# An adaLN, multi-query attention and GELU MLP block: first rows of maxima by TensorE transposes, a lead of 16 maxima in place of 24, and half of two query groups moved into the loop

## The chip, the cores and the metric

The kernel runs on one core of one Trainium2 chip, in one launch. The metric is the device time of that launch in microseconds; 1562.04 us is the median of the runs before the change.

## What is computed

The input x is 2048 rows of 512 numbers. Six modulation vectors come from `silu(c) @ w_mod`. Two sublayers follow, each on a layer norm of x with a modulation:

```python
h = layernorm(x) * (1 + ca) + sa
q = (h @ wq) in 32 heads of 16;  k = h @ wk;  v = h @ wv      # one key and one value head for all
x = x + ga * (softmax(q k^T / 4) v, heads side by side) @ wo
h = layernorm(x) * (1 + cb) + sb
x = x + gb * (gelu(h @ w1 + b1) @ w2 + b2)                     # w1: 512 x 1376
```

All is float32 outside. Inside, most factors are split into two parts of a shorter format (names ending in H and L), and a product is three matmuls: H·H, L·H, H·L.

## The kernel before

**Units.** The rows are cut into 8 blocks of 256, and the 32 heads into 8 groups of 4. A unit is one group of heads in one block: 64 units, numbered `u`, eight units to a block. For each unit the kernel needs the maximum over the keys of each score row, then the exponentials of the scores less that maximum, then their product with the values.

**Maxima.** A step of the maxima (`Max.step`) is one score product `m` on one half of the array (64 rows), and a `tensor_reduce` on VectorE that reads the 512 scores from PSUM (lines L507 and L512). A unit has 32 steps; `m` has three PSUM banks. The steps run ahead of the exponentials by a lead: `LEAD = 6` means 24 steps. `FIRST_MAX` is the order of the first 64 steps, those of units 0 and 1 (kc is the quarter of the keys). When a unit's last step is reduced, `put_max` closes the unit: VectorE reduces over the four quarters (`mm`, L560) and transposes (`turned`, L561), GpSimd gathers (`mt`, L555) and splits (`mh`, `ml`), and four small DMAs (L550) write the result into rows 48, 49, 112 and 113 of the unit's query tile `qst`. Those rows meet rows of -1 in `ks`, so that the next score product `e` (L612) has the maximum taken off, and ScalarE's exponential (L616, `p`) needs no bias. For unit 0 two of the four DMAs go through ScalarE's queue. The first `e` of a unit cannot start before these DMAs have landed.

**The loop.** After a prologue (layer norm, keys, values, the first two of sixteen query groups, `SLOTS` giving its order by hand) comes a loop of 256 iterations, four to a unit. An iteration has two half cycles; in each, TensorE issues four `e`, four `m` and, where there is one, one half of a batch of other products, and then 16 products of the exponentials with the values (`acc`, L633). Python's `clock` counts 4 to an iteration. `later(n, fn)` issues `fn` n clocks on. Every engine runs its own queue in the order in which the Python code issues, and SyncE's queue (SP) issues nearly all DMAs, in order, each waiting where it must.

**Batches.** Jobs in a queue (`put_off`) give one batch to an iteration: first the remaining query groups (`qproj_late`), then each block's output projection and MLP (`rest`, products `wops`, `tp`, `w1ps`, `w2ps`). An iteration that gets no batch is plain. The last iterations, without maxima, are called bare in the code. `rest` of block 0 can start when unit 7 is finished, its sums are fetched back and normalized; that is tied to clock 129 and what follows from it.

**Preparation of w2.** Beside this, the weights are prepared piece by piece: w1, then wo, then w2 (`prep_w2`, 11 pieces). The code for w2 starts when every query group is sent (`state["q"] == 0`), one step at the end of an iteration; while block 0's layer norm and modulation run, `busy` holds it back, and afterwards it takes two steps at a time (`turns`):

```python
if state["mods"] and state["q"] == 0 and w2H is None: ... preps["w2"] = prep_w2()
if clock[0] >= prepared[0] + PREP and weights and weights[0] in preps and not state["busy"]:
    prepared[0] = clock[0]
    for _ in range(state["turns"]):
        ... next(preps[weights[0]], 0)
```

Step i splits piece i-1 on GpSimd (L1137 and the two lines of `split`) and loads piece i+1 through SP (L1134). The last piece, number 10, is smaller than its tile, so GpSimd clears the tile first (`memset`, L1133) and its DMA waits for that.

Of the kernel before, what the change touches and what calls it, by code (L numbers as in the profile page):

```python
# [8 lines left out]
F32 = mybir.dt.float32  # L9
F32R = mybir.dt.float32r  # L10
AF = mybir.ActivationFunctionType
ALU = mybir.AluOpType
# [12 lines left out]
SLOTS = ((2, "keys 1", "keys 1"), (2, "keys 1", "keys 1"), (2, "low 1", "heads 2"), (2, "heads 2", "k 1"), (1, "warm"), (1, "heads 2"), (2, "heads 2", "v 0"),  # L25
# [4 lines left out]
MAX_WAIT = (1, 4)  # L30
QBUFS = 4
PREP = 4
BUSY = 5
# [12 lines left out]
def raw(ap):  # L46
    return ap.bitcast(F32)
# [3 lines left out]
def adaln_mqa_mlp(  # L51
# [105 lines left out]
    def mm3(ps, pairs, every=0, cost=0, begin=True, end=True):  # L157

        n, last = 0, 3 * len(pairs) - 1
        for wh, wl, xh, xl in pairs:  # L160
            for a, b_ in ((wh, xh), (wl, xh), (wh, xl)):
                nc.tensor.matmul(ps, a, b_, start=begin and n == 0, stop=end and n == last)  # L162
                n += 1
                if every and n % every == 0:
                    yield cost
# [248 lines left out]
            nc.tensor.transpose(pv_[:, t, :], vt[32:64, t * P:(t + 1) * P], ident[32:64, 32:64])  # L414
        nc.scalar.copy(va[:, b * QT:(b + 1) * QT, 0:Dh], pv_[:, :, 16:32])

    def send_q(b, g, qH, qL):
        for t, src in enumerate((qH, qL)):
            nc.sync.dma_start(out=dq[b][g][t].rearrange("a r j n -> (a r j) n"), in_=raw(src))
        state["q"] -= 1  # L420
        sent.add((b, g))

    sent = set()

    def qpairs(b, g):
        hH, hL = hts[b]
        gs = slice(g * P, (g + 1) * P)
        return [(wqH[:, k, gs], wqL[:, k, gs], hH[:, k, :], hL[:, k, :]) for k in range(KD)]

    def qtiles(b, g):  # L430
        qH = att.tile([P, BQ], F32R, name=f"qH{b}_{g}", tag="xH", bufs=2)
        qL = att.tile([P, BQ], F32R, name=f"qL{b}_{g}", tag="xL", bufs=2)
        return qH, qL

    def qproj(b, g):

        ps = psum.tile([P, BQ], F32, name=f"qps{b}_{g}", tag="v" if g else "x")
        yield from mm3(ps, qpairs(b, g), 3, 1)
        qH, qL = qtiles(b, g)
        if g == 0:  # L440
            nc.scalar.copy(qH, ps)
            nc.vector.tensor_tensor(out=qL, in0=ps, in1=raw(qH), op=ALU.subtract)
        else:
            q32 = pro.tile([P, BQ], F32, name=f"q32_{b}_{g}", tag="h32", bufs=4)
            nc.scalar.copy(q32, ps)
            split(qH, qL, q32, act, pool)
        send_q(b, g, qH, qL)
        yield -2

    def qproj_late(b, g):  # L450
        ps = psum.tile([P, BQ], F32, name=f"qps{b}_{g}", tag="x")
        size_ = BATCH if (b, g) < LONG else SHORT
        yield from batches(ps, qpairs(b, g), size_)
        q32 = wts_pool["rest"].tile([P, BQ], F32, name=f"q32_{b}_{g}", tag="ot", bufs=2)
# [4 lines left out]
        qH, qL = qtiles(b, g)  # L459
        split(qH, qL, q32, nc.gpsimd, nc.gpsimd)  # L460
        later(4, lambda: send_q(b, g, qH, qL))


    units = [(b, Q) for b in range(len(blocks)) for Q in range(NQ)]
# [3 lines left out]
    def load_q(u):  # L468

        b, Q = units[u]  # L470
        r0, w = blocks[b]
        qst = qsts[u] = qbufs[u % QBUFS]
        h, g, a0 = r0 // BQ, Q // 2, (Q % 2) * 2
        cols = slice(r0 % BQ, r0 % BQ + w)
        assert (h, g) in sent
        for s in range(2):
            for r, part in ((0, 0), (16, 1), (32, 0)):
                nc.sync.dma_start(out=raw(qst[64 * s + r:64 * s + r + 16]), in_=dq[h][g][part, a0 + s][:, :, cols])
            if u >= QBUFS:
                nc.sync.dma_start(out=raw(qst[64 * s + 48:64 * s + 50]), in_=dz)  # L480

    class Max:


        def __init__(self):
            def products(u, kcs):
                return [(u, j, t, kc) for kc in kcs for j in range(2) for t in range(blocks[units[u][0]][1] // P)]
# [5 lines left out]
            begin = [o for u, kc in FIRST_MAX for o in products(u, [kc])]  # L493
# [37 lines left out]
    def put_max(u, mx):  # L531

        T = blocks[units[u][0]][1] // P
        qst = qsts[u]
        mm = mms[u % 2]
        turned = att.tile([P, 32], F32, name=f"turned{u}", tag="turned", bufs=2)
        if u == 0:
            pad(att, 256, "pad7")  # L540
        mt = att.tile([4 * T, P], F32, name=f"mt{u}", tag="mt", bufs=2)
        mh = att.tile([4 * T, P], F32R, name=f"mh{u}", tag="mh", bufs=2)
        ml = att.tile([4 * T, P], F32R, name=f"ml{u}", tag="ml", bufs=2)

        def send():
            for s in range(2):
                for r, src in ((48, mh), (49, ml)):
                    dst = qst[64 * s + r:64 * s + r + 1].rearrange("p j (t n) -> p (j t) n", n=P)
                    ring = nc.scalar if u == 0 and s else nc.sync
                    ring.dma_start(out=raw(dst), in_=raw(src[2 * T * s:2 * T * (s + 1), :].unsqueeze(1)))  # L550
            placed.add(u)

        def gather():
            for g in range(0, P, 32):
                nc.gpsimd.tensor_scalar(out=mt[:, g:g + 32], in0=turned[g:g + 4 * T, :], scalar1=1.0, scalar2=0.0,  # L555
                                        op0=ALU.mult, op1=ALU.add)
            split(mh, ml, mt, nc.gpsimd, nc.gpsimd)

        def reduce():
            nc.vector.tensor_reduce(out=mm[:, :4 * T], in_=mx, axis=AX.X, op=ALU.max)  # L560
# [670 lines left out]
    def q_group():  # L1231
        for i in range(KD):
            next(projections[0])
            if i == KD - 1:
                next(projections.pop(0))
            yield

    def warm():
        keep_warm(WARM[2], tag="x")
        yield  # L1240

    def one(fn, *args):
        fn(*args)
        yield
# [37 lines left out]
    def last_h(t):  # L1282
        if t == QT - 1:
# [7 lines left out]
    keep_warm(WARM[1])  # L1291
    work = {"keys 1": keys(1), "heads 2": heads(2), "heads 3": heads(3), "q 1": q_group(), "keys 2": keys(2), "keys 3": keys(3),
            "v 0": one(v_out, 0), "v 1": one(v_out, 1), "v 2": one(v_out, 2), "v 3": one(v_out, 3), "rows": late_rows(),
            "low 1": one(low_k, 1), "low 2": one(low_k, 2), "low 3": one(low_k, 3), "k 1": one(repeat_k, 1), "k 2": one(repeat_k, 2), "k 3": one(repeat_k, 3), "load": one(load_q, 2), "warm": warm(),
            "wq 1": one(prep_wq, 1), "wq 2": one(prep_wq, 2), "wq 3": one(prep_wq, 3)}
    for n, *names in SLOTS:
        chunk(n)
# [9 lines left out]
    nc.scalar.copy(mod_state["rows"], mod_state["ps"])  # L1307
    put_off(*late, late_mods(), *[qproj_late(b, g) for b in range(2, NB) for g in range(KD)])
# [212 lines left out]
```

## Time and profile before

| | us |
|---|---|
| median of 3 runs | 1562.04 (1561.88 to 1562.45) |
| the profiled execution | 1561.89 |
| its span | 1560.1 |
| TensorE busy | 1543.2 (99%) |
| VectorE busy | 1400.8 (90%) |
| ScalarE busy | 1227.4 (79%) |
| GpSimd busy | 681.5 (44%) |

The profiled execution's time is 1.8 us more than its span. Lines are those of the kernel file, engines are named PE (TensorE), PEld (its weight loads), DVE (VectorE), ACT (ScalarE), POOL (GpSimd) and SP (SyncE); SPq and ACTq rows are DMA issues. A row of the timeline has a start, a duration, the engine, the line, the operation with output and input tiles, a count where several in a row are merged, and in brackets the idle time before it and what ended it.

### The profile page before, as it was taken

The numbers are of one execution on the slowest core, as the hardware profiler recorded it, in microseconds if no ns is written. First come the engines' busy times: TensorE is split into PE (matmuls) and PEld (weight loads), VectorE is DVE, ScalarE is ACT, GpSimd is POOL, SyncE is SP. The second block draws the span as 40 slices with busy tenths as digits, with TensorE's granted clock in tenths as the row PEclk, the third lists the DMA queues.
The fourth block names the chain that finished last, engine by engine and source line by source line (L and its number), as shares of the span: only waits on it lengthen the run. The fifth ranks groups of instructions, "written<-read, shape, count | busy, mean of one in ns | idle before, by whom it ended". The sixth has DMA issues, their size and how long they took to land.

```text
span 1560.1 us, 41350 instructions
## 1 busy us (share of the span) xinstructions
PE 1543.2 (99%) x16347; PEld 955.2 (61%) x16347; DVE 1400.8 (90%) x2479; ACT 1227.4 (79%) x2392; POOL 681.5 (44%) x1194
## 2 busy tenths in 40 slices
PE   7999999999999999999999999999999999999999
PEld 4456555567655665557655675556655676556657
DVE  7999999999999999999999999999999999999725
ACT  5577778788878887788877887788877888778953
POOL 5545433867322570246522562245611474225721
PEclk9999999999999999999999999999999999999999
DMA  7225412312030211202012120302112120211241
GB/s 250 92 93 197 148 56 85 124 52 97 19 109 19 83 59 36 94 28 99 30 54 76 55 86 23 109 14 100 44 49 80 46 97 17 84 55 63 84 159 52
DMA packets 83125, 121.61 MB, mean 78 GB/s; under 512 B 19614, under 2 KB 56222, under 8 KB 82676
## 3 DMA queue, kind: packets, MB, share of 16 engines
q1 hardware_dynamic: 82916, 118.97, 22.9%
q8 instruction: 129, 2.11, 0.6%
q14 instruction: 64, 0.52, 0.1%
q10 hardware_dynamic: 16, 0.00, 0.0%
HBM read 91.13 MB, written 27.27 MB: 76 GB/s over the span
## 4 chain that ended last, share of the span: by engine, by line
PE 84%; DVE 10%; issue 3%; POOL 2%; DMA 1%; ACT 1%; SPq 0%; POOLq 0%; DVEq 0%
PE acc L633 28%; PE m L507 24%; PE e L612 15%; DVE mx L512 8%; PE w1ps L193 8%; PE w2ps L183 2%; PE w1ps L183 1%; DMA xt<-in_A_x_dram 1%; PE w2ps L193 1%; PE qps L193 1%; PE tp L193 1%; PE wops L193 1%; PE kps L162 1%; DVE st L840 1%; DVE x L833 1%
## 5 line engine op out<-in xcount | busy, mean ns | idle before, releaser
L512 DVE TENSOR_REDUCE mx<-m 128x1 f32<-128x512 f32 x2048 | 1269.3, 681 | 87.7 <-PE m L507 64.7
L616 ACT ACTIVATE p<-e 128x512 f32<-128x512 f32 x2048 | 1098.0, 598 | 254.8 <-PE e L612 106.4
L507 PE MATMUL m<-ks,qst 64*128 64x512 f32 x2048 | 832.9, 429 | 2.0 <-DVE mx L512 0.6
L612 PE MATMUL e<-qst,ks 64*128 64x512 f32 x2048 | 739.9, 413 | 0.0
L633 PE MATMUL acc<-p,va 128*32 128x256 f32 x8192 | 548.0, 385 | 0.0
L507 PEld LDWEIGHTS m<-ks,qst 64*128 64x128 f32 x2048 | 367.1, 184 | 211.6 <-DVE mx L512 174.0
L612 PEld LDWEIGHTS e<-qst,ks 64*128 64x128 f32 x2048 | 358.7, 185 | 92.3 <-ACT p L616 64.0
L633 PEld LDWEIGHTS acc<-p,va 128*32 128x32 f32 x8192 | 214.5, 109 | 213.7 <-issue 110.7
L555 POOL TENSOR_SCALAR mt<-turned 8x32 f32<-8x32 f32 x256 | 53.1, 208 | 419.5 <-DVE turned L561 407.4
L193 PE MATMUL w1ps<-h2H,w1t 64*128 64x256 f32 x1216 | 232.7, 287 | 0.0
L193 PEld LDWEIGHTS w1ps<-h2H,w1t 64*128 64x128 f32 x1216 | 183.6, 185 | 28.4 <-issue 14.4
L193 PE MATMUL w1ps<-h2L,w1t 64*128 64x256 f32 x608 | 167.0, 275 | 0.0
L193 PE MATMUL w2ps<-w2H,gH 64*128 64x512 f32 x264 | 115.9, 439 | 0.0
L193 PEld LDWEIGHTS w1ps<-h2L,w1t 64*128 64x128 f32 x608 | 112.8, 185 | 0.0
L193 PE MATMUL w2ps<-w2L,gH 64*128 64x512 f32 x264 | 103.4, 392 | 0.0
L193 PE MATMUL w2ps<-w2H,gL 64*128 64x512 f32 x264 | 103.0, 390 | 0.0
L959 POOL TENSOR_SCALAR tt<-tt 128x256 f32<-128x256 f32 x77 | 31.0, 403 | 143.1 <-ACT tt L958 109.8
L137 POOL TENSOR_TENSOR gL<-z,gH 128x256 fp32r<-128x256 f32 x77 | 56.9, 739 | 6.4
L960 POOL TENSOR_TENSOR tt<-tt,z 128x256 f32<-128x256 f32 x77 | 56.8, 738 | 6.4
L970 POOL TENSOR_TENSOR z<-tt,z 128x256 f32<-128x256 f32 x77 | 56.4, 733 | 6.0
L969 POOL TENSOR_TENSOR tt<-tt,z 128x256 f32<-128x256 f32 x77 | 56.5, 734 | 0.0
L193 PE MATMUL wops<-woH,onH 64*128 64x512 f32 x112 | 49.8, 444 | 0.0
(190 smaller groups left out, 1495.3 us busy)
## 6 DMA issues: line engine op xcount, KB each, us to landing
w1t<-dw SPq DMA_DIRECT2D x82, 512.0 KB
qst<-dq SPq DMA_DIRECT2D x384, 32.0 KB
do<-oc SPq DMA_DIRECT2D x64, 128.0 KB
dw<-w1s SPq DMA_DIRECT2D x11, 512.0 KB
xt<-in_A_x_dram SPq DMA_DIRECT2D x4, 1024.0 KB
dq<-qH SPq DMA_DIRECT2D x16, 256.0 KB
dq<-qL SPq DMA_DIRECT2D x16, 256.0 KB
x<-in_A_x_dram SPq DMA_DIRECT2D x8, 512.0 KB
```

Of the source, the lines that this page charges most:

```text
L137: eng_l.tensor_tensor(out=dst_l, in0=src, in1=raw(dst_h), op=ALU.subtract)
L183: nc.tensor.matmul(ps, a, b_, start=first_, stop=last_)
L193: ins = nc.tensor.matmul(ps, a[rows], b_[rows], start=first_ and s == 0, stop=last_ and s == 1)
L507: nc.tensor.matmul(m, qsts[u][rows, j, t * P:(t + 1) * P], ks[rows, kc * 512:(kc + 1) * 512], start=True, stop=True)
L512: nc.vector.tensor_reduce(out=self.mx[u][:, i, kc:kc + 1], in_=m, axis=AX.X, op=ALU.max)
L555: nc.gpsimd.tensor_scalar(out=mt[:, g:g + 32], in0=turned[g:g + 4 * T, :], scalar1=1.0, scalar2=0.0, op0=ALU.mult, op1=ALU.add)
L612: nc.tensor.matmul(e, ks[rows, kt * P:(kt + 1) * P], rhs, start=True, stop=True)
L616: ins = nc.scalar.activation(dst, e, AF.Exp, scale=0.25)
L633: ins = nc.tensor.matmul(accs[u][32 * cidx:32 * cidx + 32, :], va[:, kt, :], rhs, start=kt == 0, stop=kt == NKT - 1)
L960: nc.gpsimd.tensor_tensor(out=tt, in0=tt, in1=z, op=ALU.mult)
L969: nc.gpsimd.tensor_tensor(out=tt, in0=tt, in1=z, op=ALU.mult)
L970: nc.gpsimd.tensor_tensor(out=z, in0=tt, in1=z, op=ALU.add)
```

## The change

- The lead is 16 steps (`LEAD = LEAD_0 = 4`), and `FIRST_MAX` puts two of unit 1's steps behind unit 0's last, which is now step 46 and not 48. Before the loop 48 steps are issued and not 56, and five idle matmuls before the loop (`WARM[3]`) are gone.
- Unit 0 is closed without GpSimd and DMAs: VectorE writes its maxima, split in two, into columns of a cleared tile `spots`, four TensorE transposes turn that into a PSUM bank, and VectorE adds the bank to `qst`.
- The other units are closed at the next half cycle: the reduction is issued 1 clock after the last step (3 before), the gather with it (1 clock later before), the DMAs 2 clocks after that (4 before). With the shorter lead the DMAs are issued at the same clock before the unit's first `e` as before.
- The first two query groups are computed in the prologue for 256 of their 512 rows only. The other halves become two more jobs of one batch each, third and fourth in the loop's queue.

```diff
-LEAD = 6
-LEAD_0 = 6
-FIRST_MAX = ((0, 0), (1, 0), (0, 1), (1, 1), (0, 2), (0, 3), (1, 2), (1, 3))
+LEAD = 4
+LEAD_0 = 4
+FIRST_MAX = ((0, 0, 4), (1, 0, 4), (0, 1, 4), (1, 1, 3), (0, 2, 4), (0, 3, 4), (1, 1, 1), (1, 2, 4), (1, 3, 4))
...
-         (0, "v 2"), (2, "q 1"), (2, "q 1"), (2, "q 1"),
-         (2, "q 1", "rows"), (2, "v 3", "wq 2"), (2, "rows"), (2, "rows"), (2, "rows", "wq 3", "load"))
-MAX_WAIT = (1, 4)
+         (0, "v 2", "q 1", "q 1", "spots"), (2, "q 1", "q 1"), (2, "q 1"), (2, "rows", "wq 2"), (2, "wq 3"),
+         (2, "rows", "load"), (2, "v 3", "rows", "first", "rows"))
+MAX_WAIT = 2
-WARM = (4, 16, 2, 5)
+WARM = (4, 16, 2, 0)
-    state = {"mods": False, "q": NB * KD, "busy": False, "turns": 1}
+    state = {"mods": False, "q": NB * KD + 2, "busy": False, "turns": 1}
...
     def qproj(b, g):
-        ps = psum.tile([P, BQ], F32, name=f"qps{b}_{g}", tag="v" if g else "x")
+        part = slice(0, HQ)
+        ps = psum.tile([P, HQ], F32, name=f"qps{b}_{g}", tag="v" if g else "x")
...
-    def qproj_late(b, g):
-        size_ = BATCH if (b, g) < LONG else SHORT
+    def qproj_late(b, g, part=slice(0, BQ)):
+        w = part.stop - part.start
+        size_ = BATCH * BQ // w if (b, g) < LONG else SHORT
...
     def put_max(u, mx):
+        if u == 0:
+            nc.vector.tensor_reduce(out=mm[:, :4 * T], in_=mx, axis=AX.X, op=ALU.max)
+            src = mm[:, :4 * T].rearrange("p (s n) -> p s n", s=2)
+            dst = spots.rearrange("p n (s c) -> p s n c", s=2)
+            nc.vector.tensor_copy(out=dst[:, :, :, 48], in_=src)
+            nc.vector.tensor_tensor(out=dst[:, :, :, 49], in0=src, in1=raw(dst[:, :, :, 48]), op=ALU.subtract)
+            return
...
-                    ring = nc.scalar if u == 0 and s else nc.sync
-                    ring.dma_start(out=raw(dst), in_=raw(src[2 * T * s:2 * T * (s + 1), :].unsqueeze(1)))
+                    nc.sync.dma_start(out=raw(dst), in_=raw(src[2 * T * s:2 * T * (s + 1), :].unsqueeze(1)))
...
-            later(MAX_WAIT[0], gather)
-            later(MAX_WAIT[1], send)
+            gather()
+            later(MAX_WAIT, send)
...
-            later((0 - clock[0]) % 4 + 1, reduce)
+            later((0 - clock[0]) % 2 + 1, reduce)
+    spots = pro.tile([P, 4, P], F32R, name="spots")
...
+    def first_rows():
+        qst = qsts[0].rearrange("p j n -> p (j n)")
+        ps = psum.tile([P, BQ], F32, name="rows0", **ebank())
+        for n in range(4):
+            nc.tensor.transpose(ps[:, n * P:(n + 1) * P], raw(spots[:, n, :]), ident)
+        nc.vector.tensor_tensor(out=qst, in0=ps, in1=raw(qst), op=ALU.add)
+        placed.add(0)
...
-    late = late[len(late) - len(projections):]
+    late = late[2:4] + [qproj_late(0, g, slice(HQ, BQ)) for g in range(2)] + late[4:]
```

More of the change, by code (lines that the diff above doesn't have):

```diff
@@ L415, in v_out, with send_q, qpairs, qtiles @@
         nc.scalar.copy(va[:, b * QT:(b + 1) * QT, 0:Dh], pv_[:, :, 16:32])
[L417 removed]
+    def send_q(b, g, qH, qL, part):
         for t, src in enumerate((qH, qL)):
[L419 removed]
+            nc.sync.dma_start(out=dq[b][g][t][:, :, :, part].rearrange("a r j n -> (a r j) n"), in_=raw(src))
         state["q"] -= 1
[L421 removed]
+        sent.update((b, g, n) for n in range(part.start, part.stop, HQ))
     sent = set()
[L425 removed]
+    def qpairs(b, g, part):
         hH, hL = hts[b]
         gs = slice(g * P, (g + 1) * P)
[L428 to L433, printed above, removed]
+        return [(wqH[:, k, gs], wqL[:, k, gs], hH[:, k, part], hL[:, k, part]) for k in range(KD)]
+    def qtiles(b, g, part):
+        w = part.stop - part.start
+        qH = att.tile([P, BQ], F32R, name=f"qH{b}_{g}_{part.start}", tag="xH", bufs=2)
+        qL = att.tile([P, BQ], F32R, name=f"qL{b}_{g}_{part.start}", tag="xL", bufs=2)
+        return qH[:, :w], qL[:, :w]
     def qproj(b, g):
[L437 to L439 removed]
+        part = slice(0, HQ)
+        ps = psum.tile([P, HQ], F32, name=f"qps{b}_{g}", tag="v" if g else "x")
+        yield from mm3(ps, qpairs(b, g, part), 3, 1)
+        qH, qL = qtiles(b, g, part)
         if g == 0:
@@ L443, in qproj @@
         else:
-            q32 = pro.tile([P, BQ], F32, name=f"q32_{b}_{g}", tag="h32", bufs=4)
+            q32 = pro.tile([P, HQ], F32, name=f"q32_{b}_{g}", tag="h32", bufs=4)
             nc.scalar.copy(q32, ps)
-            split(qH, qL, q32, act, pool)
-        send_q(b, g, qH, qL)
+            nc.scalar.copy(qH, q32)
+            yield -2
+            nc.gpsimd.tensor_tensor(out=qL, in0=q32, in1=raw(qH), op=ALU.subtract)
+        send_q(b, g, qH, qL, part)
         yield -2
-    def qproj_late(b, g):
-        ps = psum.tile([P, BQ], F32, name=f"qps{b}_{g}", tag="x")
-        size_ = BATCH if (b, g) < LONG else SHORT
-        yield from batches(ps, qpairs(b, g), size_)
-        q32 = wts_pool["rest"].tile([P, BQ], F32, name=f"q32_{b}_{g}", tag="ot", bufs=2)
+    def qproj_late(b, g, part=slice(0, BQ)):
+        w = part.stop - part.start
+        ps = psum.tile([P, w], F32, name=f"qps{b}_{g}_{part.start}", tag="x")
+        size_ = BATCH * BQ // w if (b, g) < LONG else SHORT
+        yield from batches(ps, qpairs(b, g, part), size_)
+        q32 = wts_pool["rest"].tile([P, w], F32, name=f"q32_{b}_{g}_{part.start}", tag="ot", bufs=2)
         if size_ == SHORT:
@@ L474, in load_q @@
         cols = slice(r0 % BQ, r0 % BQ + w)
-        assert (h, g) in sent
+        assert (h, g, cols.start) in sent
         for s in range(2):
@@ L490, in in_rows @@
                 return [(u, j, t, kc) for j in range(2) for t in range(blocks[units[u][0]][1] // P) for kc in range(NKC)]
-            begin = [o for u, kc in FIRST_MAX for o in products(u, [kc])]
+            parts = {(u, kc): products(u, [kc]) for u in range(2) for kc in range(NKC)}
+            begin = [parts[u, kc].pop(0) for u, kc, n in FIRST_MAX for _ in range(n)]
+            assert not any(parts.values())
             self.todo = [begin + [o for u in range(2, NU) for o in in_rows(u)] for _ in range(2)]
@@ L1234, in q_group @@
             if i == KD - 1:
-                next(projections.pop(0))
+                last = projections.pop(0)
+                next(last)
             yield
+        next(last, None)
+        yield
     def warm():
```

11 lines of the change are left out of this document (7 added, 4 removed).

## The prediction

> **What bounds the kernel now.** I read the page first, then the value products of each kind of half cycle, then the chain of waits in the last 16 us of the prologue, then the queues of POOL and SP around block 0.
>
> ```profile
> span 1560.1 us, 41350 instructions
> PE 1543.2 (99%) x16347; PEld 955.2 (61%) x16347; DVE 1400.8 (90%) x2479; ACT 1227.4 (79%) x2392; POOL 681.5 (44%) x1194
> PEclk9999999999999999999999999999999999999999
> ```
>
> PE is busy all through at a full granted clock, so an edit counts by the time it adds to or takes from PE's path. The acc products tell the length of a half cycle (16 to each), in four stretches: batches of query products, plain, batches of w1 with maxima, w1 without maxima.
>
> ```profile
> 115.80:204.21 88.41, 33.19 (x496) 12.98 (x496) 1.49 (x4) 1.00 0.49 163
> 253.38:284.73 31.35, 12.84 (x192) 5.02 (x192) 0.75 (x2) 1.00 0.35 111
> 1454.00:1471.05 17.05, 6.42 (x96) 2.52 (x96) 0.37 (x1) 1.00 0.21 71
> 1471.05:1476.24 5.19, 2.14 (x32) 0.84 (x32) 0.00 (x0) 1.00 0.02 4
> ```
>
> With query batches a half cycle takes 88.41/31 = 2.85 us, a plain one 31.35/12 = 2.61, one of w1 with maxima 17.05/6 = 2.84 and a bare one 5.19/2 = 2.60. The plain stretch is six iterations, 32 to 37: the query jobs are done, and block 0's `rest` is not ready.
>
> The end of the prologue, by the chain of waits and then the timeline:
>
> ```profile
> 64.52 0.90 PE qps L162 x3
> 65.42 1.00 PE modl L292 x8
> 66.42 0.43 PE m L507 x2
> 66.85 0.36 PE vps L414 x4
> ...
> 73.99 1.12 issue
> 75.10 0.59 ACT modl_sb L1307
> ```
>
> ```profile
> 60.62 5.22 DVE L512 TENSOR_REDUCE mx<-m 128x1 f32<-128x512 f32 x8
> 66.89 2.48 DVE L512 TENSOR_REDUCE mx<-m 128x1 f32<-128x512 f32 x4 [1.05 <-PE m L507]
> 69.40 0.19 DVE L560 TENSOR_REDUCE mm<-mx 128x8 f32<-128x32 f32 x1
> 72.62 0.58 ACTq L550 DMA_DIRECT2D qst<-ml  x1
> 75.58 4.04 ACT L616 ACTIVATE p<-e 128x512 f32<-128x512 f32 x8
> ```
>
> Unit 0's last maximum is reduced at 69.4; POOL splits it, the last DMA of its rows is issued at 72.6 through ACT's queue, and the first exponential comes at 75.58. PE fills that time with steps of unit 1 and with the five idle matmuls, which end where "issue" begins.
>
> **The prologue after the change.** Step 37 is reduced from 60.62 (what lies before keeps its length, but for the query groups below), and unit 0 now ends with step 46: ten reduces, at 2.48/4 = 0.62 each, to 66.8. PE can issue step 46 when step 43 has freed its bank, at 60.62 + 7 x 0.62 = 65.0, and is through with it at 65.3. Behind that stand 1.00 (modl), 0.43 (steps 47 and 48), 0.36 (`v 3`), 1.00 (modl), the four transposes and 1.00 (modl). Four like them, a half-width product group, a half-width copy and a full-width PSUM operation of DVE:
>
> ```profile
> 37.18 0.59 PE tp L375 x4
> 1472.90 0.89 PE w1ps L183 x6
> L645 ACT COPY oc<-acc 128x256 f32<-128x256 f32 x64 | 23.9, 373 | 5.7 <-PE acc L633 5.3
> L441 ACT CAST qH<-qps 128x512 fp32r<-128x512 f32 x1 | 0.6, 564 | 0.0
> L442 DVE TENSOR_TENSOR qL<-qps,qH 128x512 fp32r<-128x512 f32 x1 | 0.7, 693 | 1.2 <-ACT qH L441 1.2
> ```
>
> So PE ends at 65.3 + 4.38 = 69.7. DVE has `mm` and two small operations (0.2 each) done by 67.4, before the transposes want them at 68.1, then two reduces to 68.7, then the addition of 0.69 to 69.4: it hides behind the last modl. Half-width query products, 0.89 for six against 0.90 for three, lie between steps that wait for DVE, so halving them earns nothing beyond what is counted. ACT copies modl (0.59) and the first exponential stands at 69.7 + 0.1 + 0.6 = 70.4, 5.2 earlier than 75.58. Without the idle matmuls I expect the 1.12 of "issue" to go as well; if it stays (no row says what it was), the gain is 4.1. If the reduces run at 5.22/8 = 0.65, it is 5.0; at most 5.6. Earlier, group (0,0) has half the width: its cast takes 0.37 for 0.56, and ACT works there almost without a gap, so 0.2 more. **Prologue: -5.4 (-4.3 to -5.8).**
>
> **The loop.** The two moved halves take two iterations from the plain stretch (33 iterations of query batches for 31; 4 plain for 6): 4 x (2.85 - 2.61) = **+1.0**. Eight fewer steps before the loop make one bare iteration a full one: 2 x (2.84 - 2.60) = **+0.5**. The shorter lead by itself costs nothing: work per half cycle is as before, and the DMAs of a closing stand 7 clocks (10 us) ahead of the unit's first `e` as before; POOL has one clock less for the gather. Query loads and their steps shift by the same iteration. To here the sum is -3.9, or 1561.89 - 3.9 = 1558.0.
>
> **The queue behind the moved jobs.** The query jobs end two iterations later, so `prep_w2` starts two later, while block 0's layer norm keeps its clock. Before, nine pieces were done when `busy` stopped it, and two were left; now seven, and four are left. This is what the ninth step did, and what followed `busy`:
>
> ```profile
> 301.21 11.27 SPq L1134 DMA_DIRECT2D w2f<-in_B_w_dram  x2
> 312.56 0.66 SPq L550 DMA_DIRECT2D qst<-mh  x1
> 314.56 0.57 SPq L550 DMA_DIRECT2D qst<-ml  x1
> ...
> 311.58 0.53 POOL L1133 MEMSET w2f<- 128x512 f32 x1
> ...
> 329.28 0.61 ACT L900 COPY tc<-tp 128x512 f32<-128x512 f32 x1
> 328.26 1.02 POOL L555 TENSOR_SCALAR mt<-turned 8x32 f32<-8x32 f32 x4
> 330.17 0.55 POOL L907 TENSOR_SCALAR h<-tc,cb,sb 128x256 f32<-128x256 f32 x1
> 333.83 1.28 POOL L1137 TENSOR_TENSOR w2f<-w2f,gb 128x512 f32<-128x512 f32 x1
> 337.15 1.28 POOL L1137 TENSOR_TENSOR w2f<-w2f,gb 128x512 f32<-128x512 f32 x1
> 341.23 0.39 PE L612 MATMUL e<-qst,ks 64*128 64x512 f32 x1
> ```
>
> SP stood still until POOL had cleared the last tile at 312.1, and unit 11's closing DMAs went out behind it. That cost nothing, since unit 11 began late enough. After the change steps 8 and 9 both run at clock 184, right after `busy`: pieces 7 and 8, then the clearing of piece 10's tile, whose DMA stands in SP's queue just ahead of unit 12's closing (clock 185). Unit 12's first `e` is due at 341.23. In the clock of these rows: `tc` ends at 329.9; POOL modulates (333.83 - 330.17 = 3.66) to 333.6; unit 12's gather, now behind that, takes 330.17 - 328.26 = 1.91, to 335.5; two pieces at 337.15 - 333.83 = 3.32 each, to 342.2; the clearing to 342.7. SP issues piece 10 (0.4, from 312.1 to 312.56) and the four closing DMAs, the last one 2.0 after the first (314.56 - 312.56), at 345.1. A small transfer is used 1.7 to 2.2 after its issue:
>
> ```profile
> 0.72 0.45 SPq L229 DMA_DIRECT2D cc<-in_c_dram  x1
> 2.94 0.21 ACT L272 ACTIVATE ce<-cc 128x4 f32<-128x4 f32 x1 [0.94 <-DMA cc<-in_c_dram]
> SPq L767 <- DMA drs<-rsum: 8.2, 7, 1.8
> ```
>
> (2.94 - 0.72; and SP's mean wait of 8.2/7 = 1.2 behind an issue of about 0.5.) With 1.7 the last row lands at 346.8, and PE, whose queue is in order and whose first `e` is of the half that is sent last, stands **5.6** us (4.5 to 6.5). Nothing gives that back, since a half cycle is full of PE work. Behind it POOL still has two pieces ahead of the first GELU, so ACT's first tanh waits some tenths: **+0.4** (0 to 1).
>
> The sum: -5.4 + 1.0 + 0.5 + 5.6 + 0.4 = +2.1, so 1561.89 + 2.1 = **1564.0 us**. The profiled execution lies 0.15 under the median of 1562.04; against that it is +0.1%. About 0.2% (3.1 us) is what a measurement here can tell from no change.
>
> **Rivals.**
> *No stall.* If unit 12's closing does not stand behind the last w2 piece, or POOL clears the tile in time, only the front speaks: 1558.0, faster by 0.26%. For it: landings elsewhere leave room, and one stand of 10 us at SP hid completely before. Against it: the order follows from the code's clocks, and those fit the rows of before (nine pieces ahead of `busy`, two at 333.83). 0.20.
>
> *The stall slows the clock (slower).* Place: TensorE from unit 12 on. Before, PE never stood for long:
>
> ```profile
> 27.54 0.66 PE L375 MATMUL tp<-ident,xt 128*128 128x128 f32 x4 [1.25 <-ACT h L381]
> ```
>
> A wait of 1.25 us left the granted clock at 1.00; one of 5.6 has not been seen here. If it halves the clock for the length of one half cycle, work of 2.84 takes up to twice as long: up to +2.8, so 1566.8, slower by 0.3%. It decides if PE's idle time lasts long enough, which no row tells. 0.30. [...]
>
> *The front gives less.* The first exponential waits for something else (the 1.12 of "issue", the addition behind the reduces): -4.1 in place of -5.2, and with the stall 1565.1. 0.07.
>
> **How the numbers follow.** The forecast has 0.43, of which 0.35 is within 0.2% and 0.08 above it. No stall: 0.18 faster, 0.02 the same. Half clock: 0.26 slower, 0.04 the same. A smaller front: 0.03 the same, 0.04 slower. So faster 0.18, same 0.44, slower 0.38. The range goes down to 1557.8, to take in the case without a stall, and up to 1567.0 for the half clock; the forecast's own is 1562.0 to 1566.0.
>
> **What would show it.** Right: the first exponential near 70.2, 5.4 earlier; no ACTq rows of `qst`; four plain iterations in place of six before the first `wops`; an SP wait at L1134's successor for POOL's clearing, with unit 12's closing DMAs right behind it, and one idle time of 4 to 7 us on PE at unit 12's first `e`, by a DMA of `qst`. Wrong: closing DMAs of unit 12 ahead of that load; PE idle at other units' first `e`, which would make the shorter lead itself the cost; a granted clock under 1.00 behind the stall (the second rival).

## Result and the profile after

The changed kernel takes **1583.84 us** (1583.59 to 1584.12, 4 runs) against 1562.24 (1561.88 to 1562.49) for the kernel before beside it: ratio 1.0138, 95% interval 1.0121 to 1.0156. The forecast was 1564.0, its range ended at 1567.0. The profiled execution took 1583.66, its span grew from 1560.1 to 1581.8.

The head of the page after:

```profile
span 1581.8 us, 41469 instructions
PE 1556.3 (98%) x16406; PEld 963.2 (61%) x16406; DVE 1404.2 (89%) x2483; ACT 1228.8 (78%) x2392; POOL 685.2 (43%) x1193
```

The sums of work hardly differ on DVE (1404.2 for 1400.8), ACT (1228.8 for 1227.4) and POOL (685.2 for 681.5). PE's sum is 13.1 higher, but the ends of matmuls are modelled in this profile, and short waits between them are booked as busy time (359 to 361 reads 1.00 in both microseconds, though the value products there start 0.27 late); so the 21.7 us have to be followed in time. The value products mark the half cycles in both kernels, 511 of them, so the distance between the two traces can be followed from one to the next. "After minus before", worked out from the starts of the first `acc` product of each half cycle:

```
stretch                                 after - before      change
first value product (73.17, 78.68)          -5.51            -5.51
to half cycle 78 (query halves, plain)      -4.06            +1.45
79 to 94 (unit 10's first e, 1.3)           -1.76            +2.30
95 to 98 (unit 12's first e)                +6.48            +8.24
99 to 494 (50 units)                       +20.77           +14.28
last 16                                    +21.32            +0.55
```

A unit has eight half cycles (16 clocks, two to a half cycle), counted from 0, and unit j's first `e` stands in half cycle 8j - 1. Of the 14.28, 12.7 are lost in the half cycles 8j + 3, in 38 of the 50 units: six of the eight units of a block lose 0.2 to 0.5 us there, in one case 0.7 (unit 13: 0.27). A seventh (18, 26 and so on) loses 0.14 and 0.25 in the two half cycles behind it, and the eighth (15, 23 and so on) nothing; why that one is spared stays open.

**The front.** The timeline of ACT and PE at the end of the prologue after:

```profile
66.85 1.07 PE L292 MATMUL modl<-wml,csb 128*32 128x512 f32 x8
67.85 0.66 PE L594 MATMUL rows<-ident,spots 128*128 128x128 f32 x4
68.43 1.06 PE L292 MATMUL modl<-wml,csb 128*32 128x512 f32 x8
69.43 0.50 PE L639 MATMUL e<-qst,ks 64*128 64x512 f32 x2
...
70.09 4.03 ACT L643 ACTIVATE p<-e 128x512 f32<-128x512 f32 x8
```

The first exponential comes at 70.09 for 75.58 before; the transposes stand between the two last modl groups, and no idle time or "issue" is left.

**Unit 12.** SP's, POOL's and PE's timelines of after, then its windows (stretch, length, busy time of PE, PEld, DVE, ACT and POOL, then the granted clock of TensorE as a share of full speed, DMA share, GB/s):

```profile
320.94 20.25 SPq L1161 DMA_DIRECT2D w2f<-in_B_w_dram  x2
341.28 0.65 SPq L563 DMA_DIRECT2D qst<-mh  x1
343.27 0.57 SPq L563 DMA_DIRECT2D qst<-ml  x1
...
340.29 0.53 POOL L1160 MEMSET w2f<- 128x512 f32 x1
346.12 1.29 POOL L137 TENSOR_TENSOR w2L<-w2f,w2H 128x512 fp32r<-128x512 f32 x1
347.87 0.73 POOL L987 TENSOR_TENSOR tt<-tt,z 128x256 f32<-128x256 f32 x1
...
345.04 0.76 PE L639 MATMUL e<-qst,ks 64*128 64x512 f32 x1 [5.40 <-DMA qst<-ml]
```

```profile
343.00:344.00 1.00, 0.00 (x0) 0.00 (x0) 0.00 (x0) 0.00 (x0) 1.00 (x1) 0.85 0.02 4
344.00:345.00 1.00, 0.00 (x0) 0.00 (x0) 0.00 (x0) 0.00 (x0) 1.00 (x2) 0.50 0.01 2
349.00:350.00 1.00, 1.00 (x14) 0.19 (x6) 0.00 (x0) 0.31 (x1) 0.00 (x0) 0.50 0.37 63
350.00:351.00 1.00, 1.00 (x13) 1.00 (x11) 0.25 (x1) 0.71 (x3) 0.00 (x0) 0.74 0.86 287
```

SP's row of 20.25 us merges two loads of w2; the second, that of the last piece, stands until POOL has cleared the tile at 340.8. Unit 12's closing goes out behind it, and PE stands 5.40 us. The clock falls to 0.50 at 343.7 (0.85 in that microsecond) and is back at 350.5: from 345.04 on PE works 5.5 us at half speed and loses 2.7. 5.4 + 2.7 make 8.1 of the table's +8.2.

**Unit 10.** A shorter wait of the same kind stands earlier:

```profile
294.65 0.47 PE L639 MATMUL e<-qst,ks 64*128 64x512 f32 x1 [1.00 <-DMA qst<-ml]
```

The DMAs of a closing do not stand as far ahead of the unit's first `e` as before, though the code issues them at the same clock: SP sends them as soon as POOL has split the rows, whatever the code's clock (unit 13's `mh` is done at 352.55 before and 361.92 after, and the first DMA is issued at 352.58 and 361.95). Against the unit's first `e` that is later now: 11.4 us ahead before (364.02) and 8.8 after (370.79). Nearly all units have room for that: PE waits for `ml` twice in after, 5.40 and 1.00. Unit 10's go out 8.2 ahead before and 5.7 ahead after, if its wait is left out, and are slow to land: the last is issued at 290.10 and ends PE's wait at 294.65, 4.55 later, for 1.77 at unit 12 (343.27 to 345.04). The DMA share is at 0.9 to 1.0 from 288 to 294.

**The small losses.** DVE's timeline over the two half cycles around a closing, before (unit 13) and after (unit 13):

```profile
345.48 0.47 DVE L954 TENSOR_SCALAR z<-w1ps,b1c 128x256 f32<-128x256 f32 x1
345.87 3.72 DVE L512 TENSOR_REDUCE mx<-m 128x1 f32<-128x512 f32 x6
349.51 0.17 DVE L560 TENSOR_REDUCE mm<-mx 128x8 f32<-128x32 f32 x1
349.79 0.21 DVE L561 STREAM_TRANSPOSE turned<-mm 128x32 f32<-128x32 f32 x1
349.96 1.29 DVE L512 TENSOR_REDUCE mx<-m 128x1 f32<-128x512 f32 x2
...
355.66 1.29 DVE L512 TENSOR_REDUCE mx<-m 128x1 f32<-128x512 f32 x2 [0.36 <-PE m L507]
```

```profile
357.65 0.47 DVE L981 TENSOR_SCALAR z<-w1ps,b1c 128x256 f32<-128x256 f32 x1
358.05 1.28 DVE L519 TENSOR_REDUCE mx<-m 128x1 f32<-128x512 f32 x2
359.36 0.18 DVE L573 TENSOR_REDUCE mm<-mx 128x8 f32<-128x32 f32 x1
359.65 0.21 DVE L574 STREAM_TRANSPOSE turned<-mm 128x32 f32<-128x32 f32 x1
359.79 2.44 DVE L519 TENSOR_REDUCE mx<-m 128x1 f32<-128x512 f32 x4
362.45 1.29 DVE L519 TENSOR_REDUCE mx<-m 128x1 f32<-128x512 f32 x2 [0.22 <-PE m L514]
...
360.49 0.18 PEld L514 LDWEIGHTS m<-ks,qst 64*128 64x128 f32 x1
360.92 0.59 PEld L660 LDWEIGHTS acc<-p,va 128*32 128x32 f32 x16 [0.25 <-issue]
```

The last two reduces of a second half cycle are "held": the code issues them behind `z`, the GELU work of the batch. One iteration of DVE is: two reduces of the second half cycle, `z`, its two held reduces, then the four of the next first half cycle without a gap, and then 0.36 us of idling until the next second half begins. Before, `mm` and `turned` (0.45 from start to next start) stand exactly in that gap, which is gone there (349.96 has no wait). After, they stand behind the held reduces, ahead of the four: these come 0.43 later, the new unit's fourth maximum waits for a bank until 360.49, and the value products behind it start 0.27 late. Only 0.14 of the gap (0.36 to 0.22) is used.

### The profile page after: what moved, and what is told of

The parts are those of the page before. It is cut to its first block, busy times and chain, and to the rows that moved or that the text cites. A ratio compares the mean times of both kernels' runs of the same rounds, so it can differ in the third digit from the quotient of the medians.

```text
span 1581.8 us, 41469 instructions
## 1 busy us (share of the span) xinstructions
PE 1556.3 (98%) x16406; PEld 963.2 (61%) x16406; DVE 1404.2 (89%) x2483; ACT 1228.8 (78%) x2392; POOL 685.2 (43%) x1193
## 3 DMA queue, kind: packets, MB, share of 16 engines
q8 instruction: 130, 2.13, 0.6%
## 4 chain that ended last, share of the span: by engine, by line
PE 83%; DVE 6%; issue 4%; POOL 4%; DMA 2%; ACT 1%; SPq 0%; DVEq 0%; POOLq 0%; ACTq 0%
PE acc L660 28%; PE m L514 24%; PE e L639 15%; PE w1ps L193 7%; DVE mx L519 4%; PE w2ps L183 2%; PE w2ps L193 2%; PE qps L193 1%; PE w1ps L183 1%; DMA xt<-in_A_x_dram 1%; POOL w2L L137 1%; POOL w2f L1164 1%; PE tp L193 1%; PE kps L162 1%; PE wops L193 0%
## 5 line engine op out<-in xcount | busy, mean ns | idle before, releaser
L514 PE MATMUL m<-ks,qst 64*128 64x512 f32 x2048 | 842.5, 431 | 3.4 <-DVE mx L519 0.9
L514 PEld LDWEIGHTS m<-ks,qst 64*128 64x128 f32 x2048 | 368.3, 184 | 219.3 <-DVE mx L519 183.7
L193 PE MATMUL w1ps<-h2H,w1t 64*128 64x256 f32 x1232 | 237.2, 288 | 0.0
L193 PEld LDWEIGHTS w1ps<-h2H,w1t 64*128 64x128 f32 x1232 | 186.8, 185 | 29.0 <-DVE mx L519 17.7
```

The lines of the kernel that those rows point to most:

```text
L193: ins = nc.tensor.matmul(ps, a[rows], b_[rows], start=first_ and s == 0, stop=last_ and s == 1)
L514: nc.tensor.matmul(m, qsts[u][rows, j, t * P:(t + 1) * P], ks[rows, kc * 512:(kc + 1) * 512], start=True, stop=True)
```

## The experiments

All sixteen, each with its ratio to the kernel before run beside it (1562.0 to 1562.7 in the five sittings), the distance to it at the first value product, the loss between 99 and 494, and the loss at 95 to 98:

```
run                us        ratio (95%)               first acc   99-494   95-98
after            1583.84  1.0138 (1.0121-1.0156)         -5.5      +14.3     +8.2
e1_close_only    1572.80  1.0068 (1.0053-1.0083)          0.0       +6.6     +0.3
e2_lead5         1596.40  1.0219 (1.0204-1.0234)         -4.9      +25.2     +8.2
e3_clock9        1568.89  1.0043 (1.0028-1.0058)         -4.2       +1.3     +7.5
e4_send_now      1584.52  1.0142 (1.0125-1.0159)         -5.7      +13.5     +8.3
e5_gather8       1582.85  1.0129 (1.0114-1.0144)         -5.5      +14.0     +7.7
e6_turns1        1578.27  1.0097 (1.0080-1.0114)         -4.9      +14.7      0.0
e7_lead5_g6_t1   1575.16  1.0081 (1.0066-1.0096)         -4.9       +9.9     +2.2
e8_whole         1575.20  1.0081 (1.0066-1.0096)         -3.7      +13.0      0.0
e9_lead6_t1      1567.42  1.0032 (1.0019-1.0044)         -4.8       +1.7      0.0
e10_lead6_whole  1568.05  1.0036 (1.0024-1.0048)         -3.7       +0.5      0.0
e11_double       1610.39  1.0313 (1.0299-1.0327)         -5.5      +36.6     +7.9
e12_clock9_t1    1565.28  1.0017 (1.0008-1.0026)         -5.6       +1.8     +1.2
e13_mixed_t1     1563.52  1.0004 (0.9995-1.0013)         -5.5       +2.5      0.0
e14_mixed_whole  1564.59  1.0006 (0.9997-1.0015)         -3.6       +2.0      0.0
e15_front_24     1565.48  1.0013 (1.0004-1.0022)         +1.4       +0.5      0.0
e16_steps_alone  1572.62  1.0062 (1.0046-1.0079)         +0.8       +0.1      0.0
```

After, e2 to e7, e9 and e11 to e13 share one prologue; its first value product differs by up to 1.5 us between these profiled executions (-4.2 to -5.7). In e3, the -4.2, the granted clock was at 0.50 from 21.6 to 25.0.

### Where the closings stand

**e1_close_only**, from before: `later((0 - clock[0]) % 2 + 1, reduce)` for `% 4`, `gather()` at once, `later(2, send)`.

> The kernel before with one part of the change alone: a closing is reduced at the next odd clock (3 of its unit, where it was 5), gathered at once and sent 2 clocks later; lead 24 and the prologue are as before. Theory 'place' (the closing's two DVE operations, 0.18 + 0.21 us, now stand behind the two held reduces of a second half cycle, where DVE is the last, and hold up the next half cycle's third maximum by about 0.28 us in each of some 50 units): +12 to +17 us, 1574 to 1579. Theory 'lead' (16 steps of lead instead of 24 cost it, wherever the closing stands): 1562, no change. Theory 'POOL' (the gather, one clock nearer to the reduce, gets in the way of POOL's GELU work): +12 to +17, like 'place'.

Slower by 0.68%, so the earlier closing costs without a shorter lead; 'lead' as the only cause falls. Reduce, gather and send moved together here, so this run does not part DVE from POOL. The size missed: with clock 3 five of the eight units of a block lose 0.14 to 0.30 in the half cycle of their closing, 8j + 1, and three nothing (6.6 in all), and each of the first units loses 0.44, beside query batches.

**e3_clock9**, from after: `% 4 + 1` for `% 2 + 1`.

> The changed kernel with lead 16 kept, but closings reduced at the next clock that is 1 mod 4 (9 of the unit, a first half cycle) instead of 7, and sent at 11. 'Place': the losses at the half cycle 8j+3 go (-14); sending is 2 clocks (2.85 us) later, which units 10, 12, 17 and 63 with slacks of -1.2 to 2.1 us pay with 1 to 3 us each: 1572 to 1577. 'Lead' and 'POOL': no gain, 1584 to 1590.

The lead of 16 stays, the losses go (14.3 to 1.3, in the half cycles 8j + 3 from 12.7 to 0.0). DVE's timeline around unit 13's closing is that of before again, the closing behind six reduces and the gap used up:

```profile
356.93 3.73 DVE L519 TENSOR_REDUCE mx<-m 128x1 f32<-128x512 f32 x6
360.58 0.17 DVE L573 TENSOR_REDUCE mm<-mx 128x8 f32<-128x32 f32 x1
360.86 0.21 DVE L574 STREAM_TRANSPOSE turned<-mm 128x32 f32<-128x32 f32 x1
361.02 1.29 DVE L519 TENSOR_REDUCE mx<-m 128x1 f32<-128x512 f32 x2
```

It came out 3 us better than expected, since sending two clocks later cost almost nothing. What is left is mostly 0.33 at 8j + 5 in one unit of each block (18, 26 and so on), the unit that loses 0.39 in after as well.

**e2_lead5**, from after: `LEAD = 5`.

> The changed kernel with a lead of 20 steps in place of 16. Unit u+1's last maximum then falls in the first half of an iteration, so that the same rule closes it at clock 5, as in the kernel before, with the gather at once and the send at clock 7. 'Place': the 14 us of small losses go, and unit 12's closing goes out ahead of the last w2 load, so the stall and its half clock (8.2) go too: 1583.8 - 14 - 8.2 = 1561.6, 1559 to 1564. 'Lead': half of the 14 stays, 1568 to 1570. 'POOL': all of the 14 stays, 1575.

None of the three numbers came. The premise was wrong: the steps on one of the two halves of the array are done in second half cycles only, so a unit's last maximum always falls in one, and "the next half cycle" puts its closing at clock 3 or 7, never 5. It stood at 7 as in after, and a second loss was added, 0.7 to 0.9 in the half cycle 8j + 4 in three units of each block (16.3 of the 25.2 with the small ones). With this lead the unit's last reduce is not a held one, so the closing is queued ahead of the GELU work of the same clock. POOL's and ACT's timelines and PE's of this run:

```profile
361.66 1.02 POOL L568 TENSOR_SCALAR mt<-turned 8x32 f32<-8x32 f32 x4 [2.13 <-DVE turned L574]
363.56 0.39 POOL L986 TENSOR_SCALAR tt<-tt 128x256 f32<-128x256 f32 x1
...
364.81 0.42 ACT L990 ACTIVATE tt<-tt 128x256 f32<-128x256 f32 x1 [1.18 <-POOL tt L987]
...
365.77 0.49 PE L639 MATMUL e<-qst,ks 64*128 64x512 f32 x1 [0.46 <-ACT p L643]
```

POOL stands 2.13 for DVE's `turned`, GELU's `tt` comes behind the gather, ACT's tanh waits 1.18 with the exponentials behind it in order, and PE waits for those.

**e5_gather8**, from after: `later(1, gather)`. **e11_double**: `mm` and `turned` done twice.

> The changed kernel with POOL's gather one clock after the closing's reduce (8 instead of 7); DVE's two operations stay at clock 7, the send at 9. It parts DVE from POOL at clock 7, where the trace shows the new unit's fourth maximum waiting for a DVE reduce. 'DVE' (the closing's 0.4 us stand behind the two held reduces): the losses of 0.27 at half cycle 8j+3 stay, 1583 to 1586. 'POOL' (the gather ahead of GELU work, as the run with lead 20 showed at clock 5, where the last tanh waited 1.18 us for POOL): they go, 1568 to 1572.

> The changed kernel with DVE's two closing operations done twice (0.39 us more on DVE per unit, at the same clock 7; the values are the same). If DVE's time at that place is what PE waits for, nothing there absorbs more of it: +0.3 to +0.4 in each of 50 units, +15 to +20, 1599 to 1604. If the loss is a fixed wait (for a semaphore, for POOL), 1584 to 1588.

e5 changes nothing that counts (14.0): at clock 7 it is not POOL. e11 is slower by 26.6: of that 22.3 (36.6 - 14.3) between 99 and 494, 0.3 to 0.5 in nearly every unit, 0.45 in the mean, those without a loss in after among them. DVE's timeline around a closing of e11:

```profile
362.66 0.19 DVE L573 TENSOR_REDUCE mm<-mx 128x8 f32<-128x32 f32 x1
363.55 2.44 DVE L519 TENSOR_REDUCE mx<-m 128x1 f32<-128x512 f32 x4
```

The reduces begin 0.89 behind `mm`, for 0.43, so the second pair takes 0.46 on DVE, and all of it is passed on to PE, a little more than I expected. In the waits the same shows as one line in four kernels (before, after, e3, e11: engine, line, what released it: total us, times, longest):

```profile
PEld m L507 <- DVE mx L512: 174.0, 439, 0.8
```

```profile
PEld m L514 <- DVE mx L519: 183.7, 464, 0.8
```

```profile
PEld m L514 <- DVE mx L519: 175.8, 443, 0.8
```

```profile
PEld m L514 <- DVE mx L519: 209.2, 493, 1.0
PE m L514 <- DVE mx L519: 16.7, 44, 0.5
```

174.0 before, 183.7 with the closing at clock 7, 175.8 with it at clock 9, 209.2 and a row of 16.7 (0.9 in after) with the doubled work.

**e7_lead5_g6_t1**, from after: `LEAD = 5`, `later(1, gather)`, `later(4, send)`, and `turns` left at 1.

> The changed kernel with lead 20 (closing at clock 5), the gather one clock later (6) and the send at 9, as in the kernel before, and one step of w2 per due time. 'Place' (only where the closing's operations stand in DVE's and POOL's queues costs, not the lead): no small losses, no stall: 1562.0 - 4.9 (first product 4.9 earlier in the run with lead 20) + 1.0 + 0.5 + 0.5 = 1559.1, 1557.5 to 1561. 'Lead': 1566 or more.

It missed by 14 at least, being planned on e2's wrong premise: the closing stays at clock 7, and 8.5 us stay in the half cycles 8j + 3. Gather and send moved later together take away e2's second loss (16.3 to 0.9 in 8j + 4), which fits POOL's part there.

### Unit 12

**e4_send_now**, from after: `send()` for `later(MAX_WAIT, send)`.

> The changed kernel, but the four DMAs of a closing are issued right behind its gather (clock 7) instead of 2 clocks later, which puts unit 12's ahead of the last w2 load in SP's queue. All theories of the small losses: they stay. The stall at unit 12 (5.4 us) and the half clock behind it (2.8 us) go: 1583.8 - 8.2 = 1575.6, 1574 to 1577. If the stall had another cause (POOL late with the rows, or the transfer itself), 1582 to 1584. SP stands longer for POOL in every unit; if that delays loads of w1 or q rows, 1577 to 1580.

The rows went out at 335.86 to 338.5, ahead of the load, and the stall stayed. SP's, POOL's, ACT's and PE's timelines:

```profile
337.91 0.57 SPq L563 DMA_DIRECT2D qst<-ml  x1
...
350.55 0.72 POOL L987 TENSOR_TENSOR tt<-tt,z 128x256 f32<-128x256 f32 x1
...
351.31 0.42 ACT L990 ACTIVATE tt<-tt 128x256 f32<-128x256 f32 x1 [6.18 <-POOL tt L987]
...
352.26 0.79 PE L639 MATMUL e<-qst,ks 64*128 64x512 f32 x1 [5.99 <-ACT p L643]
```

Two waits of nearly one length lay side by side: the closing's DMAs, and ACT's first tanh, which waits for POOL's four w2 pieces. Taking away one shows the other. Unit 10 paid as well: there PE stood 2.55 us for a residual add, with a fall of the clock behind it.

**e6_turns1**, from after: `state.update(busy=False)` without `turns=2`. **e8_whole**, from after: `part = slice(0, BQ)` in `qproj`, no halves in `late`.

> The changed kernel, but after the first layer norm of the MLP one step of w2 is done per due time (every 4 clocks) instead of two. Sending unit 12's rows early left the time as it was, since then the exponentials stood 6.0 us behind a tanh that waited for four w2 pieces on POOL (335.7 to 350). 'Backlog' (both the closing's DMAs and the first GELU wait for POOL's row of w2 pieces): now unit 12's closing is ahead of the clearing and one piece at a time stands before GELU: the stall and its half clock go, -7 to -8.4, 1575 to 1577. If only the DMAs' queue counted: the same here. If w2 comes too late for the second MLP product of block 0: up to 10 us later, 1580 to 1590.

> The changed kernel with the first two query groups projected whole in the prologue and no halves left to the loop. Then the w2 steps keep the clocks of the kernel before (nine pieces before the layer norm). Expected: front 0 to 0.3 later than with halves, two plain iterations back (-1.0), no stall (-8.2), the 14 us of small losses stay: 1583.8 - 8.2 - 1.0 + 0.2 = 1574.8, 1573.5 to 1576. If halving was what earned the front, the first value product moves from 72.9 to 74 or later and the time is 1576 to 1577.

Both free unit 12 (0.0 at 95 to 98): in e6 the pieces are spread and the closing goes out before the clearing, in e8 two pieces are left instead of four. e6 came 1.3 us above its range: in the profiled execution unit 10's first `e` waited 3.28 for its `ml` rows (1.00 in after), with a fall of the clock behind it (0.50 from 297.2 to 300.6). e8 is at its number, but not by its sum: its first value product is at 75.02 for 73.17, so halving earns about 1.8 in the front, which I had put at 0 to 0.3, and the half cycles up to 78 and the small losses gave that back (1.0 for 1.45, and 13.0 for 14.3). The three executions with whole groups and 16 steps (e8, e10, e14) lie at -3.6 to -3.7, those with halves at -4.2 to -5.7.

### The front

**e9_lead6_t1**, from after: `LEAD = 6` (`LEAD_0` stays 4), `% 4 + 1`, gather 1 and send 4 clocks later, `turns` left at 1. **e10_lead6_whole**: the same with whole groups and `turns=2`.

> The changed prologue (first rows by transposes, 16 steps ahead at its end, half of the first two query groups left to the loop) in front of the loop of the kernel before (lead 24, closings at the next clock that is 1 mod 4, gather one clock and send four clocks later), and one step of w2 per due time. Sum: 1562.2 - 5.2 + 1.0 + 0.5 = 1558.5, 1557.5 to 1560.5; growing the lead from 16 to 24 over the first units may cost up to 1 more. If it is not below 1561, the front's gain is lost elsewhere and the account is wrong.

> The same with the two query groups whole in the prologue (first value product at 74.8 in the run with whole groups, 3.65 earlier than before, instead of 5.5) and w2 as in the changed kernel: 1562.2 - 3.7 + 0.5 = 1559.0, 1558 to 1561. Halving then earns about 1.8 in the front and pays 1.0 for the two longer iterations.

Both missed by 9: slower than before. From the first value product to half cycle 40 they lose 5.7 and 7.2. The lead grows by 8 steps over the first units, and six half cycles with five maxima take 3.30 for 2.84 (2.8 in all). Unit 4's first `e` waits for its rows, 1.67 in e9 and 1.84 in e10; half cycles 31 and 32 lose 1.9 and 3.6 there, in e10 with the clock at 0.50 from 167.9 to 171.3. The rest, 1.0 and 0.8, lies in half cycles beside these. They raised the question what the front's gain consists of.

**e15_front_24**: e10 with `LEAD_0 = 6`; the order of the prologue's other work stays that of after, without idle matmuls. **e16_steps_alone**, from before: `LEAD_0 = 4` and no steps in the last two slots.

> The loop of the kernel before (lead 24, closings at clocks 5, 6 and 9), whole query groups in the prologue, and 24 steps done ahead at the end of the prologue instead of 16; what is left of the change is the first rows by transposes. 'Steps' (the front's gain is mostly the 8 steps, each a DVE reduce of 0.62, that the prologue leaves out): the first value product comes 8 x 0.62 = 5.0 later than the 74.7 with 16 steps, at 79 to 80; no growing of the lead (which cost 5.7), so 1562 to 1563.5. 'Transposes' (the gain is the way of the rows through TensorE instead of through POOL and DMA): at 75 to 76, and 1559 to 1560.

> The kernel before with 16 steps done ahead in the prologue instead of 24, and nothing else: unit 0's rows still go through POOL and DMA, whole query groups, the lead grows to 24 over the first units (which cost 5.7 in the run that did so). What counts is the start of the first value product, 78.4 before. 'Together' (the rows land at about 75 whatever PE does, so the 8 steps lay beneath that wait and leaving them out earns nothing without the transposes): 77.4 to 78.4. 'Steps alone': 73.4. The time is then 1567 to 1568, or 1562 to 1563.

Without the 8 steps left out (e15) the first value product comes 1.36 later than before; the steps alone (e16) bring it 0.75 later. In the front 'Steps' came for e15 (80.04), and for e16 'Together', 1 us over its 78.4 (79.43; 78.68 before). The times came neither way: e15 took 1565.48, 2 us above its range, and e16 1572.62, 4.6 above, with 8.4 lost from the first value product to half cycle 40, where the lead grows and unit 4's first `e` waits 2.46. DVE's and ACT's timelines of e15, then PE's of e16:

```profile
71.95 9.69 DVE L519 TENSOR_REDUCE mx<-m 128x1 f32<-128x512 f32 x16 [0.73 <-PE m L514]
...
76.34 3.56 ACT L643 ACTIVATE p<-e 128x512 f32<-128x512 f32 x7 [4.16 <-PE e L639]
```

```profile
75.27 0.56 PE L612 MATMUL e<-qst,ks 64*128 64x512 f32 x2 [2.93 <-DMA qst<-ml]
```

In e15 the rows are there early, but the first `e` stands on PE behind 8 steps that DVE reduces without a gap: e8's 75.02 and 8 x 9.69/16 make 79.9. In e16 the steps are gone and PE stands for the DMA; the clock is at 0.50 from 77.3 to 80.8, which can take about 1 of the time to its first value product. Two covers lay over each other, and only the change of both gives a gain: 3.7 with whole groups (e8), 5.5 with the halves. The halves alone were not run.

### Together

**e12_clock9_t1**: e3 and e6. **e13_mixed_t1**: the same, units 10 and 12 closed at clock 7, `send()` at once. **e14_mixed_whole**: e13 with whole groups and `turns=2`.

> The changed kernel with its lead of 16 kept, closings at clock 9 (behind a first half cycle) and one step of w2 per due time. 'Place': no small losses and no long stall: 1568.9 - 7.4 = 1561.5, 1560 to 1563.5. If the lead of 16 itself costs, more than 1565.

> The changed kernel with lead 16, closings at clock 9 but for units 10 and 12 (7), sent right behind the gather, one step of w2 per due time. From the profiled run with closings at clock 9 and one step of w2 (+0.7 at its last product against before): units 10 and 12 give back 1 to 2.5, so -1 to -2: 1560 to 1561.5. If unit 10 still waits for its rows: 1562 to 1564.

> The same with whole query groups in the prologue and two steps of w2 per due time, as before. Front 3.7 earlier, no moved halves (-1.0), two w2 pieces in the backlog instead of four: 1562.2 - 3.7 + 0.5 + 1.8 (the half cycle 8j+5 of one unit per block) = 1560.8, 1560 to 1562.

None came at its first number. e12 was announced as showing a cost of the lead itself above 1565, and it came at 1565.28; its eleven runs lie between 1562.6 and 1568.2, and the profiled one, at 1563.68, loses 2.7 in the half cycles in which units 10 and 12 begin (1.5 and 1.2). e13 came in the range given for the case that unit 10 still waits for its rows, but not by them: PE waits there 0.91 for a residual add on DVE. e14 is 2.6 above its range, with 1.49 of the same wait. With both repairs the lead of 16 and the new front come to 1563.5 (e13), 1.3% under the changed kernel and not to be told from the kernel before (0.9995 to 1.0013). No version here beats it. In e13 the front's 5.5 are used up by the moved halves and what lies beside them (+1.3 to half cycle 78), the half cycle of unit 10's first `e` (1.3) and 0.5 about it, 0.5 at half cycle 99, 0.33 in one unit of each block at 8j + 5 (2.0), and the end (0.8). The 2.0 do not come from clock 9: with lead 16 or 20 these half cycles lose 1.3 to 2.2 in all at any of the places, with lead 24 (e9, e10, e15) 0.3 at most. So the shorter lead may itself cost up to 2 us; by what stays open.

## Why the prediction was wrong

- **The step that failed:** "The shorter lead by itself costs nothing: work per half cycle is as before, and the DMAs of a closing stand 7 clocks (10 us) ahead". I checked the DMAs' time and POOL's clock, not where DVE's two operations land. They moved from clock 5 to 7, out of the only gap of an iteration, and cost 13.0 of the 14.3 us over 50 units. Shown by e1 (the earlier closing alone is slower), e3 (moved to clock 9 at the same lead, 14.3 to 1.3), e5 (not POOL) and e11 (doubled, passed on in full). Of the lead itself at most about 2 us are left, in e12 and e13, which keep it. My line of what would show it wrong named idle PE at other units' first `e`; the loss lay at their fifth half cycle instead. The half sentence on the DMAs failed too: 11.4 us ahead became 8.8 at unit 13, and unit 10 waited 1.00.
- **The stall at unit 12** was right in place and cause, 5.40 for 5.6. But its end was bound twice: the "+0.4" for POOL's pieces ahead of the first tanh stood for a second wait as long as the first (e4). In after the two overlap, and the term itself measured 0.1 (8.2 less 5.4 and 2.7).
- **The clock** did what the second rival said: half speed, 2.7 us for "up to +2.8". That a wait would halve it was my assumption, which no row of before showed; in after it is at 0.50 from 343.7 to 350.5, 6.8 us. The fall comes 4.1 us into the wait of 5.40 (339.64 to 345.04), and the 5.5 us at half speed hold 2.75 of work, close to the one half cycle (2.84) I had taken. PE's longest wait before was not the 1.25 but 8.26, ahead of its first matmul, and the granted clock reads 1.00 from 0 to 16.
- **The front**: -5.51 for -5.4, the first exponential at 70.09 for 70.4, the 1.12 of "issue" gone. That the number came is partly luck: the sum gives 5.2 to the transposes and the steps and 0.2 to the halves, and the runs give 3.7 (e8) and 1.8. Neither the transposes nor the steps earn anything alone (e15, e16).
- **The loop's small terms**: +1.45 for +1.0 up to half cycle 78, +0.55 for +0.5 at the end. The moved halves took 0.9 of the 1.45 (half cycles 46 to 49 and 63 to 66); most of the rest is the first small losses, at units 1, 6, 7 and 9. Not foreseen: unit 10, whose first `e` comes 1.3 late; its rows had landed only 0.4 us ahead of that `e` before.

So -5.4 + 1.0 + 0.5 + 5.6 + 0.4 became -5.5 + 1.5 + 0.5 + 8.2 + 2.3 + 14.3 = +21.3, and 0.4 behind the last value product. The 2.3 are unit 10 and units about it (half cycles 79 to 94).

## What to carry to other kernels

When a step moves in a schedule that is full, look for the gap that absorbed it on each engine it uses, in the trace and at that clock: 0.45 us on DVE cost nothing in one half cycle and 0.2 to 0.5 in the next, in 38 of 50 units. A wait that is removed can hide another of the same length (5.40 and 5.99 us at unit 12), and a saving can need two covers lifted together (the front, 5.5 us), so test both alone and both together before putting a price on either.

## What the runs showed of the hardware that I had not expected

The clock fell after short waits too. In e4 PE stood 2.55 us for the residual add at unit 10, and its windows show the granted clock at 0.50 from 295.5 to 298.9:

```profile
295.00:296.00 1.00, 0.37 (x2) 0.37 (x4) 1.00 (x2) 0.00 (x0) 1.00 (x2) 0.75 1.01 332
297.00:298.00 1.00, 1.00 (x8) 0.73 (x6) 1.00 (x2) 0.75 (x2) 0.95 (x1) 0.50 1.04 428
298.00:299.00 1.00, 1.00 (x10) 0.35 (x10) 0.70 (x2) 0.34 (x1) 0.35 (x1) 0.54 0.99 381
```

After waits of 1.84 (e10), 2.46 and 2.93 (e16), 2.55 (e4) and 3.28 (e6) the clock stayed at 0.50 for 3.4 us, after waits of 4.54 (e5) to 5.99 (e4, unit 12) for 6.8; waits of 1.0 to 1.67 (e9) left it at 1.00. So a fall stands behind a wait of 1.84 (e10), and none behind the 8.26 ahead of the first matmul (before).

Nor did every fall come behind one long wait. In e15 the clock was at 0.50 from 74.76 to 81.59, though PE's waits in the 3.4 us before that were 0.55 at most and 0.85 in all. In e3's prologue it was at 0.50 from 21.6 to 25.0, behind waits of 0.90 at most. PE's timeline and a window of e15:

```profile
72.70 3.18 PE L514 MATMUL m<-ks,qst 64*128 64x512 f32 x5 [0.55 <-DVE mx L519]
76.00:78.00 2.00, 2.00 (x9) 1.18 (x8) 2.00 (x5) 1.66 (x4) 0.00 (x0) 0.50 0.00 0
```

PE went there at DVE's pace in e15, one `m` for each reduce of 0.61 us. Whether that pace made the clock fall no run here shows.
